# The output product of the last two row groups of an attention kernel, as three one-pass products of exact parts

## The chip, the core and the metric

The kernel runs on one core of one Trainium2 chip. The core has five engines with a queue each: TensorE (PE in the profile, its weight loads PEld), VectorE (DVE), ScalarE (ACT), GpSimd (POOL) and SyncE (SP), which issues most transfers. Each engine works through its own instructions in order and waits on semaphores for the others. Products land in PSUM, eight banks of 128 x 512 float32; everything else lies in SBUF or in device memory. The metric is device microseconds (us) of one execution; lower is better.

## What is computed

Two attention layers over 2048 rows with 576 columns, 32 heads of 18, side by side in the output. Layer A has one key and value head for all 32 query heads and no mask; layer B works in four segments of 512 rows with a memory carried from one to the next.

```python
def _A_ref(x, wq, wk, wv, wo):
    q = (x @ wq).reshape(B, S, H, Dh).transpose(0, 2, 1, 3)
    k = x @ wk
    v = x @ wv
    scores = jnp.einsum("bhqd,bkd->bhqk", q, k) * (Dh ** -0.5)
    p = _softmax(scores, axis=-1)
    o = jnp.einsum("bhqk,bkd->bhqd", p, v)
    return o.transpose(0, 2, 1, 3).reshape(B, S, H * Dh) @ wo
...
return jnp.concatenate([a, b], axis=-1)
```

The change concerns the last line of layer A, the product of the weighed heads with `wo` (576 x 576), for the last two of its four groups of 512 rows.

## The kernel before

A first phase projects both inputs. It splits every float32 operand into a rounded part (`hi`, type float32r) and the exact rest (`lo`), and sums three products, hi x hi, lo x hi, hi x lo, each of which passes through TensorE once (`proj` at line 249, and `values` at line 491, where each product has 128 weight columns taken from the input and 288 or 306 columns of the weights as the moving side). A branch that the drawn inputs do not take follows, and then the attention loop.

The attention loop interleaves scores (L925, L934), exponentials (L943 on ScalarE, some on VectorE) and products with the values (L973). Behind it runs a list of steps that fall due by round: `at` puts a step on the list, `due` emits those whose round `k` has come. For every group of 512 rows, `finish` puts on it: a load of the softmax sums (`sums`, L713, tile `sm`), their reciprocal on VectorE and its store (`inverses`, L726, L731), loads of the raw heads (`load_heads`, L738, tile `o`, two buffers), loads of the inverses (`load_inverses`, L745, tile `rb`) and the multiplication of the heads by them on GpSimd (`weigh`, L758). The 576 head columns are held as five pieces t = 0 to 4, four of 126 rows and one of 72. The last piece holds the last four heads, whose sums come last.

When a group is weighed, its output product `out_proj` joins the list `fill`. It multiplies in plain float32, with 32 weight columns at a time on four column strips of TensorE (`out_part`, L770), 192 output columns per bank and twelve banks per group, each summed over the five pieces; a copy on VectorE takes a bank to the tile `osb` (L795, two buffers) and every third copy is followed by a store (`out_store`, L781). One group is 60 steps (`FILL`). In the attention loop one step runs per round.

What is left at the end of the loop (the rest of the last B group, and the third A group) runs in the ending, eight steps per round, and the last A group follows through all eight banks: six halves of the three tiles `E`, one `O` and one `F`, 288 output columns each, first the pieces 0 to 3 of every bank, then piece 4, then eight copies on ScalarE and VectorE in turn and four stores from tiles of the name `P`.

In this part the order of TensorE, ScalarE and VectorE is the order in which the code emits the instructions (`manual_schedule`, L1093). SyncE's queue is in order too; a tile that is allotted again waits until its last use is over, a store among them.

Of the kernel before, what the change touches and what calls it, by code (L numbers as in the profile page):

```python
# [7 lines left out]
F32 = mybir.dt.float32  # L8
F32R = mybir.dt.float32r
# [3 lines left out]
ALU = mybir.AluOpType  # L13
# [5 lines left out]
S, D, H, DH = 2048, 576, 32, 18  # L19
NSEG, L = 4, 512  # L20
C = 512
# [3 lines left out]
RT = [18 * h for h in HT]  # L25
# [5 lines left out]
PBUFS = 9  # L31
# [40 lines left out]
def attention_pair_kernel(ctx, tc, a_xT, a_w, a_wo, b_xT, b_w, b_wo, b_beta, ident_d, hmask_d, bmask_d, cmask_d, sel_d, zmask_d, selx_d, sely_d, out):  # L72
    nc = tc.nc
# [79 lines left out]
    with ExitStack() as ph:  # L153
# [106 lines left out]
        for c in range(NCH):  # L260
            ready = {}
            if c == 0:
# [11 lines left out]
                for k in range(5):  # L274
# [3 lines left out]
                    for i, (w, x) in enumerate(parts_):  # L278
                        for t in TILES:
# [5 lines left out]
                                start=k == 0 and i == 0,  # L285
# [9 lines left out]
            for t in TILES:  # L295
# [8 lines left out]
                R = RT[t]  # L304
# [54 lines left out]
        for t in range(5):  # L359
            R = RT[t]  # L360
# [405 lines left out]
    def out_part(ab, c, i, t, dst, c0, n, start, stop):  # L766

        for j in range(4):
            r0 = 128 * i + 32 * j
            nc.tensor.matmul(  # L770
                dst[32 * j : 32 * j + 32],
                parts[ab, c][: RT[t], t, r0 : r0 + 32],
                wo[ab][: RT[t], t, c0 : c0 + n],
                start=start,
                stop=stop,
            )

    def out_store(ab, c, i, osb):
        r0 = c * C + 128 * i
        col = 0 if ab == "A" else D  # L780
        nc.sync.dma_start(out[r0 : r0 + 128, col : col + D], osb)  # L781

    def out_proj(ab, c):

        for i in range(4):
            osb = pa.tile([128, D], F32, name="osb", bufs=2)
            for q in range(3):
                cs = slice(192 * q, 192 * q + 192)

                pf = psO.tile([128, C], F32, name="O" if ending and (3 * i + q) % 2 else "F")  # L790
                for t in range(5):
                    out_part(ab, c, i, t, pf[:, :192], cs.start, 192, t == 0, t == 4)
                    if t < 4:
                        yield False
                nc.vector.tensor_copy(osb[:, cs], pf[:, :192])  # L795
                if q == 2:
                    out_store(ab, c, i, osb)
                yield True
# [50 lines left out]
                at(now[0] + 2, 0, lambda: True, store)  # L849
                yield True  # L850

    fill, filled, ending = [], [0], []

    def run_fill(n, whole=False):

        done = 0
        while done < n and fill:
            try:
                full = next(fill[0])
            except StopIteration:  # L860
                fill.pop(0)
                continue
            done += 1
            filled[0] += 1
            if full and not whole:
                break
        return done


    blocksA = [("A", c, hg) for c in range(NCH) for hg in range(8)]  # L870
# [145 lines left out]
    def at(k, cost, ready, step):  # L1016
        later.append((k, cost, ready, step))
        later.sort(key=lambda e: e[0])

    def due(k, most=2, heavy=2):  # L1020

        cost = 0

        near = [its[n][0] for t in turns[k : k + 3] for n, pr in t]
        heavy *= "B" not in near
        for e in [e for e in later if e[0] <= k]:
            if most and cost + e[1] <= heavy and e[2]():
                later.remove(e)
                e[3](k)
                cost += e[1]  # L1030
                most -= 1
        return cost

    def finish(k, ab, c, hg):

        ts = range(4) if hg == 6 else range(4, 5)
        lo, hi = (0, 28) if hg == 6 else (28, 32)
        box, need = {}, 3 if ab == "B" and c > 0 else 1
        weighed.setdefault((ab, c), 0)
        last = (ab, c) == blocks[-1][:2]  # L1040

        d0, d1, d2, d3 = (0, 2, 0, 3) if last else (2, 5, 3, 5) if (ab, c) == ("B", 0) else (2, 5, 3, 6)

        def begin(k):
            assert ab == "A" or c not in LATE_ASK or asked[0] >= c
            summing.add(hg)
            box[0] = sums(ab, c, lo, hi)
            at(k + d1, 0, lambda: True, inv)

        def inv(k):  # L1050
            inverses(ab, c, lo, hi, box[0])
            summing.remove(hg)
            for t in ts:
                at(k, 0, place, lambda k, t=t: load(k, t))

        def place():

            return (ab, c) in parts or len(parts) - filled[0] // FILL < 2 and asked[0] >= min(2, len(parts) + 1)

        def load(k, t):  # L1060
            load_heads(ab, c, t)
            at(k + d2, 0, room, lambda k: weights(k, t))

        def room():

            return loaded[0] + need <= 10

        def weights(k, t):
            loaded[0] += need
            tiles = load_inverses(ab, c, t)  # L1070
            box[t, t] = weigh(ab, c, t, tiles)
            at(k + d3, 1, lambda: True, lambda k: heads(k, t))

        def heads(k, t):
            box[t, t].pop(0)()
            if box[t, t]:
                at(k, 1, lambda: True, lambda k: heads(k, t))
                return
            loaded[0] -= need
            weighed[ab, c] += 1  # L1080
            if weighed[ab, c] == 5 and not last:
                at(k + 2, 0, lambda: True, lambda k: fill.append(out_proj(ab, c)))

        at(k + d0, 0, lambda: hg not in summing, begin)

# [7 lines left out]
    with tc.manual_schedule(engines={ENG.PE, ENG.Activation, ENG.DVE}):  # L1093

        for n, b in enumerate(blocks):
            ms = [m for m in range(len(its)) if block_of[m] == n]
            items = [(m, k) for m in ms for k in range(2)]
            for out_, cut in ((turns, len(items) // 3), (prods, len(items) // 3 - 2)):  # L1100
                at_ = split(len(items), cut)
                out_ += [items[a:z] for a, z in zip(at_, at_[1:])]
        at(ASK + 4, 0, lambda: True, lambda k: load_qf(2))
        for k in range(len(turns) + 2):
            now[0] = k
            exps = [scores(its[n], pr, i == 1) for i, (n, pr) in enumerate(turns[k])] if k < len(turns) else []
            for i in (0, 2, 1) if len(exps) == 3 else range(len(exps)):
                exps[i]()
            if memory is None:
                run_fill(1)  # L1110
            elif k >= ASK and all(its[n][0] == "A" for n, pr in turns[k]) and next(memory, None) is None:
                memory = None

            ends = k > 1 and any(hf and its[n][3] == (NKT - 1 if its[n][0] == "A" else 2) for n, hf in prods[k - 2])
            if slow and (slow[0][0] <= k or not ends):
                slow.pop(0)[2]()
            for n, hf in prods[k - 2] if k > 1 else []:
                ab, c = its[n][:2]
                hg = products(its[n][:3], its[n][3], hf)
                if hg in (6, 7):  # L1120
                    finish(k, ab, c, hg)
                if hg == 7 and ab == "B" and c + 1 < NSEG:
                    load_vseg(c + 1)
            due(k)
            for n, pr in turns[k] if k < len(turns) else []:
                it = its[n]
                ab = it[0]
                if pr == 0:
                    prefetch(ab, keys[ab].index((ab, it[1], it[2] // 2)) + 2)
                    if it in (("A", 0, 2, 8), ("A", 0, 5, 8)):  # L1130
                        load_wo(*(("B", b_wo) if it[2] == 2 else ("A", a_wo)))

        ab, c = blocks[-1][:2]
        ending.append(True)
        while fill:
            due(k, 4)
            run_fill(8, whole=True)
            k += 1
        while weighed[ab, c] < 4:
            due(k, 4)  # L1140
            k += 1
        banks = [psE.tile([128, 2, 512], F32, name="E") for _ in range(3)]
        dst = [bk[:, hf, :288] for bk in banks for hf in range(2)]
        for nm in ("O", "F"):
            bk = psO.tile([128, C], F32, name=nm)
            dst.append(bk[:, :288])
        for g in range(8):
            for t in range(4):
                out_part(ab, c, g // 2, t, dst[g], 288 * (g % 2), 288, t == 0, False)
        while later:  # L1150
            due(k, 4)
            k += 1
        for g in range(8):
            out_part(ab, c, g // 2, 4, dst[g], 288 * (g % 2), 288, False, True)
        for i in range(4):
            osb = pp.tile([128, 2, 512], F32, name="P", bufs=PBUFS)
            for hf in range(2):
                (nc.vector.tensor_copy if hf else nc.scalar.copy)(osb[:, hf, :288], dst[2 * i + hf])
            out_store(ab, c, i, osb[:, :, :288])


# [54 lines left out]
```

## Time and profile before

| | us |
|---|---|
| median of 3 runs | 1428.38 (1427.50 to 1430.46) |
| profiled execution, its time | 1427.14 |
| profiled execution, its span | 1425.4 |
| TensorE busy in the span | 1410.3 |
| ScalarE busy | 1195.2 |
| VectorE busy | 1022.9 |
| GpSimd busy | 247.0 |

The span is what the trace covers; the time also holds what lies around it. Rows of the order of time have the start in us from the span's start, the length in us, the engine, the line of the kernel, the operation, output<-inputs, the shapes, how many instructions were merged, and in brackets the idle time of the engine just before with what ended it. Rows of groups end with busy time in us and mean ns of one, and then the idle time before them. In the trace a float32 product shows as two records, a float32r product as one. The end of a product is modelled; the distance of two starts is what one costs in a stream. SPq rows are the issue of a transfer, not its length.

### The profile page before, as it was taken

The page shows a single profiled execution, that of the slowest core. Times are in us where ns is not written, and L with a number is a line of the kernel's source. Part 1 is how long each engine was busy: PE and PEld are TensorE (multiplying, and loading weights), DVE is VectorE, ACT ScalarE, POOL GpSimd, SP SyncE. Part 2 cuts the span into 40 slices and gives each one's busy share as a digit, 9 for nine tenths or more (in the row PEclk, how much of TensorE's full clock was granted, in tenths as well). Part 3 has the DMA queues.
Part 4 walks back from the last instruction along what each step waited for, and adds up shares of the span by engine and source line. Part 5 has one row for each costly group of instructions (what it writes and reads, how often), then busy time and mean ns, then how long its engine had stood idle before and what let it go on. Part 6 is the DMA issues. An engine that isn't in the chain of part 4 may idle for free.

```text
span 1425.4 us, 41103 instructions
## 1 busy us (share of the span) xinstructions
PE 1410.3 (99%) x17692; PEld 839.5 (59%) x17692; DVE 1022.9 (72%) x1213; ACT 1195.2 (84%) x1429; POOL 247.0 (17%) x326
## 2 busy tenths in 40 slices
PE   9999999999999999999999999999999999999998
PEld 6788888755555555555555555555555555555565
DVE  6556456467787778777777888777778877877761
ACT  4543434489999999999999999999999999999960
POOL 2431000003313214131111150131013300200001
PEclk9999999999999999999999999999999999999999
DMA  9866546457564535232322532231105121110022
GB/s 275 261 215 188 168 143 226 161 165 230 158 202 159 170 109 175 87 108 77 102 68 66 175 118 86 85 114 64 36 34 151 48 78 51 51 43 18 18 87 77
DMA packets 90469, 172.71 MB, mean 121 GB/s; under 512 B 14576, under 2 KB 22377, under 8 KB 89854
## 3 DMA queue, kind: packets, MB, share of 16 engines
q1 hardware_dynamic: 83722, 159.75, 35.8%
q0 software_dynamic: 1664, 4.78, 1.3%
q10 hardware_dynamic: 4896, 5.51, 1.2%
q8 instruction: 140, 2.29, 0.7%
q14 instruction: 47, 0.39, 0.1%
HBM read 99.32 MB, written 70.67 MB: 119 GB/s over the span
## 4 chain that ended last, share of the span: by engine, by line
PE 66%; ACT 9%; issue 2%; DVE 1%; DMA 0%; POOL 0%; DVEq 0%; ACTq 0%
PE O L973 30%; PE E L925 19%; PE F L770 11%; ACT P L943 9%; PE E L934 3%; PE E L770 1%; PE F L827 1%; PE O L770 1%; DVE W L940 1%; DMA out<-osb 0%; DVE osb L795 0%; DVE q L905 0%; DVE q L902 0%; POOL P L948 0%; DVE o L832 0%
## 5 line engine op out<-in xcount | busy, mean ns | idle before, releaser
L943 ACT ACTIVATE P<-E 128x1024 f32<-128x1024 f32 (+1 forms) x800 | 783.3, 1065 | 12.1 <-PE E L925 12.0
L940 DVE COPY W<-E 128x1024 f32<-128x1024 f32 (+1 forms) x384 | 461.2, 1201 | 177.9 <-PE E L925 120.6
L973 PE MATMUL O<-P,VA 128*32 128x256 f32 x7936 | 508.5, 380 | 0.0
L943 ACT ACTIVATE P<-W 128x1024 f32<-128x1024 f32 (+1 forms) x384 | 429.1, 1117 | 2.4 <-DVE W L940 2.2
L973 PEld LDWEIGHTS O<-P,VA 128*32 128x32 f32 x7936 | 262.7, 110 | 146.5 <-issue 5.7
L925 PE MATMUL E<-stA,kstA 56*128 56x512 f32 x1920 | 328.4, 439 | 1.1 <-ACT P L943 0.4
L925 PEld LDWEIGHTS E<-stA,kstA 56*128 56x128 f32 x1920 | 154.9, 184 | 176.3 <-ACT P L943 110.2
L948 POOL TENSOR_SCALAR_AFFINE_SELECT P<-P 128x256 f32<-128x256 f32 (+1 forms) x192 | 94.6, 493 | 474.4 <-ACT P L943 441.5
L758 POOL TENSOR_TENSOR o<-o,rb 126x512 f32<-126x512 f32 (+1 forms) x55 | 81.2, 1490 | 410.7 <-PE F L770 142.2
L770 PE MATMUL F<-woB,o 126*32 126x192 f32 (+1 forms) x1920 | 127.4, 338 | 0.3 <-DVE osb L795 0.3
L905 DVE SCALAR_TENSOR_TENSOR q<-q,PD 128x1024 f32<-128x1024 f32 x96 | 119.3, 1243 | 0.0
L973 PE MATMUL O<-P,vseg 128*32 128x256 f32 (+2 forms) x1536 | 81.4, 344 | 0.0
L770 PEld LDWEIGHTS F<-woB,o 126*32 126x32 f32 (+1 forms) x1920 | 38.2, 108 | 70.8 <-issue 62.4
L770 PE MATMUL F<-woA,o 126*32 126x192 f32 (+1 forms) x1240 | 77.7, 338 | 0.6 <-DVE osb L795 0.6
L982 DVE COPY oe<-O 128x512 f32<-128x512 f32 x64 | 44.3, 692 | 42.6 <-PE O L973 41.2
L118 ACT CAST qp<-pj 126x512 fp32r<-126x512 f32 (+1 forms) x54 | 30.9, 584 | 49.9 <-DVE kmB L447 32.7
L249 PE MATMUL pj<-xh,wBl 128*126 128x512 f32 x180 | 72.3, 403 | 0.0
L249 PE MATMUL pj<-xh,wBh 128*126 128x512 f32 x180 | 71.8, 400 | 0.0
L119 DVE TENSOR_TENSOR qp<-pj,qp 126x512 fp32r<-126x512 f32 (+1 forms) x54 | 36.6, 686 | 37.3 <-ACT qp L118 37.2
L934 PE MATMUL E<-stB 56*128 56x256 f32 (+3 forms) x512 | 61.7, 348 | 1.6 <-ACT P L943 1.1
L973 PEld LDWEIGHTS O<-P,vseg 128*32 128x32 f32 x1536 | 48.8, 109 | 24.3 <-issue 1.6
L934 PEld LDWEIGHTS E<-stB 56*128 56x128 f32 x512 | 38.6, 185 | 32.0 <-ACT P L943 22.3
(182 smaller groups left out, 1366.3 us busy)
## 6 DMA issues: line engine op xcount, KB each, us to landing
stB<-kB SPq DMA_DIRECT2D x96, 144.0 KB
stB<-qB SPq DMA_DIRECT2D x32, 288.0 KB
stA<-qA SPq DMA_DIRECT2D x30, 288.0 KB
oA<-oe SPq DMA_DIRECT2D x32, 256.0 KB
oB<-oe SPq DMA_DIRECT2D x32, 256.0 KB
qA<-qp SPq DMA_DIRECT2D x16, 504.0 KB
kB<-qp SPq DMA_DIRECT2D x16, 504.0 KB
qB<-qp SPq DMA_DIRECT2D x16, 504.0 KB
```

Source lines behind the costliest of these rows:

```text
L119: hold(nc.vector.tensor_tensor(qp[:R, 1, :n], src, qp[:R, 0, :n].bitcast(F32), op=ALU.subtract))
L249: nc.tensor.matmul(dst, w[:, c0 : c0 + M], x, start=i == 0, stop=i == len(ops) - 1)
L758: return lambda: tc.keep_in_program_order(nc.gpsimd.tensor_tensor(dst, a, b, op=op))
L770: nc.tensor.matmul(dst[32 * j : 32 * j + 32], parts[ab, c][: RT[t], t, r0 : r0 + 32], wo[ab][: RT[t], t, c0 : c0 + n], start=start, stop=stop,
L905: steps.append(lambda a=a: v.scalar_tensor_tensor(q, q, a, p, op0=ALU.add, op1=ALU.mult))
L925: nc.tensor.matmul(e[:, j], kstA[rows, 128 * kt : 128 * kt + 128], st[rows, h, :], start=True, stop=True)
L934: nc.tensor.matmul(e[:, j, c0 : c0 + 512 - 128 * k], st[rows, 4 + h, ks], st[rows, h, 128 * k :], start=True, stop=True)
L940: nc.vector.tensor_copy(src[:, :, :n], e[:, :, :n])
L943: nc.scalar.activation(p[:, :, :n], src[:, :, :n], AF.Exp, scale=SCALE)
L948: nc.gpsimd.affine_select(diag, diag, pattern=[[0, 2], [0, m], [1, 128]], base=0, channel_multiplier=-1, compare_op=ALU.is_ge, fill=0.0)
L973: nc.tensor.matmul(o[32 * j : 32 * j + 32, q0 : q0 + n], v, p[:, j % 2, p0 : p0 + n], start=m == hf == 0, stop=last and hf == 1,)
L982: nc.vector.tensor_copy(osb, o)
```

## The change

The ending is rewritten. The group that is under way when the loop ends is finished one step per round of the due list. All groups behind it, here the third and the fourth of layer A, go through a common path:

- the weights `wo` of layer A are split into hi and lo parts, piece by piece, in two tiles of the name `stB`;
- each piece of the weighed heads is split likewise into the two halves of a `P` tile: hi by a copy on ScalarE, lo by a subtraction on VectorE;
- for each piece and each of the eight banks three products follow, 128 rows of the group as weights and 288 columns of `wo` moving;
- eight copies on ScalarE and VectorE in turn take the banks to four tiles, named `W` (two buffers, `bufs=2`) for the third group and `P` for the last, and four stores follow;
- then the next group does the same in the same eight banks.

```diff
-                pf = psO.tile([128, C], F32, name="O" if ending and (3 * i + q) % 2 else "F")
+                pf = psO.tile([128, C], F32, name="F")
...
-        ending.append(True)
-        while fill:
+        while fill and fill[0][0] in begun:
             due(k, 4)
-            run_fill(8, whole=True)
+            run_fill()
+            if filled[0] % FILL == 0:
+                fill.pop(0)
             k += 1
...
+        rows = [key for key, steps in fill] + [blocks[-1][:2]]
+        wparts = [pa.tile([128, 8, C], F32R, name="stB", bufs=2) for _ in range(2)]
+        wh, wl = (w.rearrange("p a b -> p (a b)")[:, : 5 * D].rearrange("p (t d) -> p t d", d=D) for w in wparts)
...
+        def halve(hi, lo, src):
+            nc.scalar.copy(hi, src)
+            nc.vector.tensor_tensor(lo, src, hi.bitcast(F32), op=ALU.subtract)
...
+        def halve_heads(key, t):
+            R = RT[t]
+            x = halves_of[key, t] = pp.tile([128, 2, 512], F32R, name="P", bufs=PBUFS)
+            halve(x[:R, 0], x[:R, 1], parts[key][:R, t])
...
+        def multiply(key, t, dst):
+            R = RT[t]
+            x = halves_of[key, t]
+            for g in range(8):
+                i, c0 = g // 2, 288 * (g % 2)
+                for m, (xp, w) in enumerate(((0, wh), (1, wh), (0, wl))):
+                    nc.tensor.matmul(
+                        dst[g],
+                        x[:R, xp, 128 * i : 128 * i + 128],
+                        w[:R, t, c0 : c0 + 288],
+                        start=t == m == 0,
+                        stop=t == 4 and m == 2,
+                    )
...
+        for n, key in enumerate(rows):
+            end = key == rows[-1]
+            banks = [psE.tile([128, 2, 512], F32, name="E") for _ in range(3)]
+            dst = [bk[:, hf, :288] for bk in banks for hf in range(2)]
+            dst += [psO.tile([128, C], F32, name=nm)[:, :288] for nm in ("O", "F")]
+            for t in range(5):
+                R = RT[t]
+                if n == 0:
+                    halve(wh[:R, t], wl[:R, t], wo["A"][:R, t])
+                if end:
+                    while weighed[key] <= t:
+                        due(k, 4)
+                        k += 1
+                else:
+                    due(k, 4)
+                    k += 1
+                halve_heads(key, t)
+                multiply(key, t, dst)
+            for i in range(4):
+                osb = pp.tile([128, 2, 512], F32, name="P" if end else "W", bufs=PBUFS if end else 2)
+                for hf in range(2):
+                    (nc.vector.tensor_copy if hf else nc.scalar.copy)(osb[:, hf, :288], dst[2 * i + hf])
+                out_store(*key, i, osb[:, :, :288])
```

`run_fill` now runs one step of the first entry of `fill` and records in `begun` which group has been started; its calls in the attention loop do what they did.

More of the change, by code (lines that the diff above doesn't have):

```diff
@@ L850, in ask_memory, with run_fill @@
                 yield True
[L852 to L867, printed above, removed]
+    fill, filled, begun = [], [0], set()
+    def run_fill():
+        while fill:
+            key, steps = fill[0]
+            if next(steps, None) is not None:
+                begun.add(key)
+                filled[0] += 1
+                return
+            fill.pop(0)
     blocksA = [("A", c, hg) for c in range(NCH) for hg in range(8)]
@@ L1081, in heads @@
             if weighed[ab, c] == 5 and not last:
-                at(k + 2, 0, lambda: True, lambda k: fill.append(out_proj(ab, c)))
+                at(k + 2, 0, lambda: True, lambda k: fill.append(((ab, c), out_proj(ab, c))))
         at(k + d0, 0, lambda: hg not in summing, begin)
@@ L1109, in attention_pair_kernel @@
             if memory is None:
-                run_fill(1)
+                run_fill()
             elif k >= ASK and all(its[n][0] == "A" for n, pr in turns[k]) and next(memory, None) is None:
@@ L1131, in attention_pair_kernel @@
                         load_wo(*(("B", b_wo) if it[2] == 2 else ("A", a_wo)))
-        ab, c = blocks[-1][:2]
-        ending.append(True)
-        while fill:
+        while fill and fill[0][0] in begun:
             due(k, 4)
-            run_fill(8, whole=True)
+            run_fill()
+            if filled[0] % FILL == 0:
+                fill.pop(0)
             k += 1
[L1139 to L1159, printed above, removed]
+        rows = [key for key, steps in fill] + [blocks[-1][:2]]
+        assert all(ab == "A" for ab, c in rows)
+        wparts = [pa.tile([128, 8, C], F32R, name="stB", bufs=2) for _ in range(2)]
+        wh, wl = (w.rearrange("p a b -> p (a b)")[:, : 5 * D].rearrange("p (t d) -> p t d", d=D) for w in wparts)
@@ new lines, in halve @@
+        def halve(hi, lo, src):
+            nc.scalar.copy(hi, src)
+            nc.vector.tensor_tensor(lo, src, hi.bitcast(F32), op=ALU.subtract)
+        halves_of = {}
+        def halve_heads(key, t):
[15 more added lines that the diff above has]
+                    )
@@ L1163 @@
+        assert not later
 def kernel(A_x, A_wq, A_wk, A_wv, A_wo, B_x, B_wq, B_wk, B_wv, B_wo, B_beta):
```

## The prediction

> **What bounds the kernel now.** I read the head of the page first, then the chain of waits, then the last 50 us in order of time, because the edit touches nothing earlier: up to the last products of the attention loop both programs have the same instructions in the same order on every engine.
>
> ```profile
> span 1425.4 us, 41103 instructions
> PE 1410.3 (99%) x17692; PEld 839.5 (59%) x17692; DVE 1022.9 (72%) x1213; ACT 1195.2 (84%) x1429; POOL 247.0 (17%) x326
> PE 66%; ACT 9%; issue 2%; DVE 1%; DMA 0%; POOL 0%; DVEq 0%; ACTq 0%
> ```
>
> TensorE (PE) sets the time. Everything that the change can win or lose therefore lies where TensorE's own stream gets shorter or stops. The stage in question, in order of time (columns: start, length, engine, line, output<-inputs, count, and the idle time before with its releaser):
>
> ```profile
> 1376.09 1.22 ACT L943 ACTIVATE P<-W 128x1024 f32<-128x1024 f32 x1
> ...
> 1379.63 1.16 PE L770 MATMUL F<-woB,o 126*32 126x192 f32 x24
> 1379.88 0.69 DVE L982 COPY oe<-O 128x512 f32<-128x512 f32 x1 [3.58 <-PE O L973]
> 1380.60 0.34 SPq L984 DMA_DIRECT2D oA<-oe  x1
> ...
> 1381.04 0.76 SPq L738 DMA_DIRECT2D o<-oA  x1
> ...
> 1381.36 1.83 PE L770 MATMUL F<-woA,o 126*32 126x192 f32 x40 [0.57 <-DVE osb L795]
> 1381.85 0.45 SPq L781 DMA_DIRECT2D out<-osb  x1
> 1382.35 0.76 SPq L738 DMA_DIRECT2D o<-oA  x1
> ...
> 1383.21 0.56 SPq L713 DMA_DIRECT2D sm<-oA  x1
> ...
> 1388.60 1.28 POOL L758 TENSOR_TENSOR o<-o,rb 126x512 f32<-126x512 f32 x1 [0.81 <-DMA o<-oA]
> 1388.75 0.25 DVE L726 RECIPROCAL sm<-sm 128x16 f32<-128x16 f32 x1 [0.25 <-DMA sm<-oA]
> ...
> 1390.33 1.28 POOL L758 TENSOR_TENSOR o<-o,rb 126x512 f32<-126x512 f32 x1 [0.45 <-DMA o<-oA]
> ...
> 1398.60 1.26 POOL L758 TENSOR_TENSOR o<-o,rb 72x512 f32<-72x512 f32 x1 [5.55 <-DMA rb<-rA]
> ...
> 1401.41 11.82 PE L770 MATMUL E<-woA,o 126*32 126x288 f32 x192
> ...
> 1420.33 0.67 PE L770 MATMUL F<-woA,o 72*32 72x288 f32 x8
> 1420.52 0.46 DVE L1158 COPY P<-E 128x288 f32<-128x288 f32 x1 [0.46 <-ACT P L1158]
> 1420.58 0.40 ACT L1158 COPY P<-O 128x288 f32<-128x288 f32 x1
> 1421.06 0.46 DVE L1158 COPY P<-F 128x288 f32<-128x288 f32 x1
> ```
>
> The last B group ends on TensorE at 1380.8. The third A group ("A2") runs from 1381.36 to 1401.41, 20.1 us, the fourth ("A3") to 1421.0, 19.6 us; 4.4 us of copy and store end the span. Note the reciprocal at 1388.75: VectorE waited there for the load of the last softmax sums, 8 us after their source was stored. Before, TensorE had 20 us of A2 to do meanwhile, fed by copies that stand ahead of that reciprocal in VectorE's order.
>
> **What the products become worth.** Each group loses its full-precision products on 32 columns and gets 5 x 8 x 3 = 120 one-pass products of 128 weight columns by 288. The first phase has exactly that kind (two weight parts, two input parts, new weights for every product), and their starts give the price:
>
> ```profile
> 159.09 0.30 PE L491 MATMUL pj<-wBh,xl 128*128 128x288 f32 x1
> ...
> 165.09 0.29 PE L491 MATMUL pj<-wBl,xh 128*128 128x288 f32 x1
> ...
> L491 PEld LDWEIGHTS pj<-wBl,xh 128*128 128x128 f32 x160 | 30.1, 188 | 0.2 <-issue 0.2
> ```
>
> Between the first two rows lie 45 starts, so 6.00 / 45 = 0.133 us each, whatever the 0.3 us of one by itself. A group is 120 x 0.133 = 16.0 us, a piece t (24 products) 3.2 us. Gain on TensorE: 20.1 + 19.6 - 32.0 = 7.7 us. That is all that the change can win.
>
> [...] The rows above show a load of 0.188 us for every product and starts 0.133 us apart, so the loads are hidden there.
>
> **What stands ahead of the first product: the first stall.** Each product needs rounded parts: ScalarE rounds (hi), VectorE subtracts (lo). ScalarE is free at 1376.09 + 1.22 = 1377.3 and its two roundings for t = 0 (0.68 and 0.62) are done by 1378.7, hidden under the last B products. The subtractions are not hidden. In the written order of the engines the tail now runs one output step per round of the due list, not eight, so the reciprocal of the last sums is emitted ahead of the last B copy and of every subtraction. Queued behind that one wait on VectorE are the B copy, ten subtractions, and through them TensorE's second product.
>
> When do the sums land? SyncE's queue changes: the store of 288 KB that stood between the first two loads of A3's heads moves behind the reciprocal, and three head loads of 252 KB now stand ahead of the load of the sums, where there were two and that store. An earlier instance with an empty queue and the landing before bound it:
>
> ```profile
> 1355.73 0.85 SPq L713 DMA_DIRECT2D sm<-oA  x1
> ...
> 1358.27 0.94 DVE L726 RECIPROCAL sm<-sm 112x128 f32<-112x128 f32 x1
> ```
>
> Issue stays near 1383.3 (three issues of 0.76 after 1381.04). Lower bound 1383.3 + 2.5 = 1385.9; upper, behind the third head load and the fourth's share, 1391. Before, the sums landed just behind the second head load (1388.60); with a third load in place of a store of about the same size I take between that and the third's landing (1390.33): 1389.5.
>
> Behind it VectorE does reciprocal 0.25, B copy 0.36, and the first two subtractions, by the nearest rows:
>
> ```profile
> L211 DVE TENSOR_TENSOR xl<-wBl,xh 128x512 fp32r<-128x512 f32 x7 | 4.7, 689 | 5.7 <-ACT xh L205 5.6
> L223 DVE TENSOR_TENSOR wAl<-wBl,wAh 128x618 fp32r<-128x618 f32 x5 | 3.9, 803 | 0.0
> L239 ACT CAST wBh<-wr 128x576 fp32r<-128x576 f32 x5 | 3.4, 680 | 0.0
> L205 ACT CAST xh<-wBl 128x512 fp32r<-128x512 f32 x5 | 3.1, 620 | 4.7 <-DMA wBl<-a_xT 4.7
> ```
>
> 0.75 for 576 columns (between the two rows) and 0.69 for 512: 2.05 us, and 0.15 to reach TensorE (osb ended at 1381.22, its reader began at 1381.36). TensorE resumes at 1389.5 + 2.05 + 0.15 = 1391.7. It has stood since 1380.9 but for one product: 10.8 us. Pieces t = 1 to 4 cost VectorE 1.44 us against 3.2 on TensorE, so they are hidden.
>
> **The clock.** What a stop does to TensorE is shown by the end and the start of the span (columns of the first: window, us, busy of PE, PEld, DVE, ACT, POOL, granted clock, DMA share, GB/s):
>
> ```profile
> 1421.00:1422.00 1.00, 0.00 (x0) 0.00 (x0) 0.46 (x1) 0.00 (x0) 0.00 (x0) 1.00 0.90 316
> 1422.00:1423.00 1.00, 0.00 (x0) 0.00 (x0) 0.00 (x0) 0.00 (x0) 0.00 (x0) 0.84 1.06 372
> 1423.00:1424.00 1.00, 0.00 (x0) 0.00 (x0) 0.00 (x0) 0.00 (x0) 0.00 (x0) 0.50 0.56 198
> ...
> 1.54 4.02 PE L168 MATMUL nd<-sht 128*128 128x512 bf16 x9 [1.54 <-DVE gt L469]
> ...
> 6.51 1.19 PE L281 MATMUL pj<-xh,wAh 128*114 128x512 f32 x4 [0.95 <-ACT wAh L222]
> ```
>
> The clock is halved 1.7 us after the last product (0.84 is 0.68 us at 1.00 and the rest at 0.50). At the start nine products take 4.02 us, 0.45 each, where four of the same width take 1.19 later. So after a stop about 4 us run at half speed: a loss of 2.0 us, bounds 0 and, if it lasts 7 us, 3.5.
>
> [...]
>
> A2 then ends on TensorE at 1391.7 + 15.9 (119 products) + 2.0 = 1409.6.
>
> **The second stall.** A3 uses the same eight banks, and A2's eviction stands ahead of A3's rounding on ScalarE and VectorE. The output tiles are now "W", of which there are two for four stores, so the third pair of copies waits until the first store has been read out; the change adds that wait. The first pair of banks is complete 18 products before the end, 1407.2, and about 0.3 us later visible. In the old ending a pair took 0.98 us from its ScalarE copy to the store's issue:
>
> ```profile
> 1418.21 0.40 ACT L1158 COPY P<-E 128x288 f32<-128x288 f32 x1 [40.90 <-PE E L770]
> 1418.71 0.46 DVE L1158 COPY P<-E 128x288 f32<-128x288 f32 x1 [16.69 <-ACT P L1158]
> ...
> 1419.19 2.77 SPq L781 DMA_DIRECT2D out<-P  x4
> ...
> 1394.87 7.51 SPq L781 DMA_DIRECT2D out<-osb  x3
> ...
> 1399.34 0.36 DVE L795 COPY osb<-O 128x192 f32<-128x192 f32 x1 [2.62 <-DMA out<-osb]
> ```
>
> So the first store goes out at 1408.5, the second 0.8 later at 1409.3. From issue to reuse, a store took 1399.34 - 1394.87 = 4.5 us with another load ahead of it; the last four stores, issued by 1421.6, ended with the span, under 3.8. I take 3.7. The second tile is free at 1413.0; ScalarE copies (0.40) and rounds A3's first piece (0.62), VectorE copies and subtracts (0.69), 1.85 us with the hand-overs: TensorE resumes at 1414.8, 5.2 us after A2. Without the wait for the tiles it would be 1.5. At 5.2 us the clock falls again: 2.0.
>
> A3's own pieces were weighed early, its last one, 11.1 us after the reciprocal (1398.60 + 1.26 against 1388.75), at 1400.6; needed near 1428, so hidden.
>
> **The sum.** 1414.8 + 15.9 + 2.0 = 1432.7; 0.2 to the modelled end and 4.4 of copy and store as before: 1437.3, against 1425.4: +11.9 us. In terms: -7.7 for products, +10.3 for the first stall (1391.7 against 1381.36), +5.2 for the second, +4.0 for the clock, rest roundings. The profiled execution took 1427.14 us, 1.7 more than its span; 1427.14 + 11.9 = 1439.0. The median of the runs shown, 1428.38, is 1.2 higher, so I add half of that: 1439.5.
>
> **The rivals.**
> 1. *The clock stays full across the second stop*, 5.2 us being not long enough, or both losses are small. For it: the record at the start shows 1.00 even though the cadence is half, so the column is not a sure guide. Against: the fall within 1.7 us. One loss less: 1437.5, 18%; both gone: 1435.5, 7%.
> 2. *VectorE isn't held* (the other side): if the subtractions came ahead of the reciprocal's wait, TensorE would resume near 1382.8, with no cold clock there: 8.9 + 2.0 less, 1439.5 - 10.9 = 1428.6, no change. It decides at a start of the A2 products before about 1385. For it speaks only that the sums of an idle queue came in 2.5 us; even so the start would be 1388.1. Chance 5%, with 2% for a result faster than before, where the tiles' wait goes too (1423).
> 3. *The transfers are later*: sums behind all five head loads (1391.8), stores at 4.5 us, half speed for 7 us: +2.3 +0.8 +1.5 to 3: 1445. For it: the head loads in these rows land 1.7 us apart, and the queue is full. Chance 12%.
> 4. *Weight loads show*: if the load's 0.188 us were added to every product, 240 x 0.188 = 45 us more: 1485. The 45 starts speak against it: 1%. [...]
>
> **How the numbers follow.** The forecast with both stalls and both clock losses has 57%, centre 1439.5. The bounds of the landing (-3.6, +1.5), of the stores (-0.4, +0.8) and of the clock (-4, +3) don't all fall together; with rival 1 inside, 1434.5 to 1444.0 leaves out rivals 2 and 4 and most of 3, under 2 in 10. 0.2%, what a measurement can tell from no change here, is 2.9 us: faster 2%, same 4%, slower 94%.
>
> **What would show it.** In the profile after: a gap on TensorE of about 10 us ahead of the first products of stB and P, ended by VectorE, behind a reciprocal that a DMA ended; starts 0.133 us apart once warm and 0.25 just after the gaps; granted clock near 0.5 there; a second gap of 4 to 6 us, with ScalarE's third copy into W ended by the DMA that stores W. Wrong would be: the first of these products running through before 1385, no wait of that copy, or starts 0.2 us apart and more throughout.

## The result and the profile after

| | us |
|---|---|
| before, median of 4 runs | 1429.10 (1427.50 to 1430.46) |
| after, median of 4 runs | 1441.18 (1438.04 to 1441.63) |
| ratio | 1.008, 95% interval 1.0062 to 1.0099 |
| profiled execution after: time, span | 1441.63, 1439.9 |

The change makes the kernel 12 us slower, 0.8%, and the interval leaves out 1. The forecast was 1439.5, with 1434.5 to 1444.0.

The head of the page after the change (busy time, share of the span, instructions), with the row of the granted clock in 40 slices:

```profile
span 1439.9 us, 40019 instructions
PE 1407.7 (98%) x17132; PEld 847.2 (59%) x17132; DVE 1036.6 (72%) x1220; ACT 1204.8 (84%) x1448; POOL 248.8 (17%) x326
PEclk9999999999999999999999999999999999999989
```

TensorE is busy for 2.6 us less than before and the span is 14.5 us longer, so it stands still for longer than before. The last 60 us in order of time, columns as before:

```profile
1383.59 1.16 PE L770 MATMUL F<-woB,o 126*32 126x192 f32 x24
...
1384.56 0.34 SPq L978 DMA_DIRECT2D oA<-oe  x1
1384.68 0.40 PE L1156 MATMUL E<-stB,P 126*128 126x288 f32 x1
1385.00 2.56 SPq L738 DMA_DIRECT2D o<-oA  x3
1387.66 0.56 SPq L713 DMA_DIRECT2D sm<-oA  x1
1392.74 0.25 DVE L726 RECIPROCAL sm<-sm 128x16 f32<-128x16 f32 x1 [8.21 <-DMA sm<-oA]
1393.04 2.99 POOL L758 TENSOR_TENSOR o<-o,rb 126x512 f32<-126x512 f32 x2 [0.39 <-DMA o<-oA]
1393.12 1.80 DVE L1141 TENSOR_TENSOR stB<-woA,stB 126x576 fp32r<-126x576 f32 x1
1394.84 1.75 DVE L1141 TENSOR_TENSOR P<-o,P 126x512 fp32r<-126x512 f32 x1
1396.51 0.75 DVE L1141 TENSOR_TENSOR stB<-woA,stB 126x576 fp32r<-126x576 f32 x1
1396.64 4.19 PE L1156 MATMUL E<-stB,P 126*128 126x288 f32 x17 [11.56 <-DVE P L1141]
1397.18 0.68 DVE L1141 TENSOR_TENSOR P<-o,P 126x512 fp32r<-126x512 f32 x1
1401.47 2.55 PE L1156 MATMUL E<-stB,P 126*128 126x288 f32 x18
...
1404.66 2.56 PE L1156 MATMUL E<-stB,P 126*128 126x288 f32 x18
...
1413.04 4.12 SPq L781 DMA_DIRECT2D out<-W  x4
...
1415.35 0.40 ACT L1185 COPY W<-E 128x288 f32<-128x288 f32 x1 [2.04 <-DMA out<-W]
...
1417.89 3.85 PE L1156 MATMUL E<-stB,P 126*128 126x288 f32 x17 [0.33 <-DVE P L1141]
...
1422.38 2.56 PE L1156 MATMUL E<-stB,P 126*128 126x288 f32 x18
```

The first product, which needs hi parts alone, runs at 1384.68. The next waits 11.56 us for VectorE, whose own wait of 8.21 us is for the load of the last sums, at the reciprocal. Behind it the first two subtractions take 1.80 and 1.75 us while GpSimd multiplies, the next two 0.75 and 0.68. The starts of two pieces, 1401.47 and 1404.66, are 3.2 us apart. The piece just after the stop takes 4.8 (1396.64 to 1401.47, less one product). At 1415.35 ScalarE's third copy has waited 2.04 us for the store out of `W`, and A3's stream begins at 1417.89. Its first piece takes 4.5 us. The granted clock in windows (window, us, busy of PE, PEld, DVE, ACT, POOL, clock, DMA share, GB/s):

```profile
1388.00:1390.00 2.00, 0.00 (x0) 0.00 (x0) 0.00 (x0) 0.00 (x0) 0.00 (x0) 1.00 0.45 175
1390.00:1391.00 1.00, 0.00 (x0) 0.00 (x0) 0.00 (x0) 0.00 (x0) 1.00 (x1) 0.57 0.46 164
...
1396.00:1398.00 2.00, 1.36 (x5) 1.36 (x6) 2.00 (x4) 0.00 (x0) 0.04 (x1) 0.50 0.08 28
...
1417.00:1418.00 1.00, 0.51 (x2) 0.30 (x2) 0.86 (x2) 1.00 (x3) 0.00 (x0) 0.72 0.85 298
1418.00:1419.00 1.00, 1.00 (x4) 1.00 (x5) 1.00 (x3) 1.00 (x3) 0.00 (x0) 0.50 0.90 308
```

The clock is halved at 1390.1, 5 us after TensorE stopped, and again at about 1417.4, 3 us after the second stop began. Both streams start at half speed.

Below, "the ending" is the time from the start of the last B products (here 1383.59) to the end of the span; it leaves out what varies ahead of it. It grew from 45.8 us (1425.4 - 1379.63) to 56.3, by 10.5.

### The profile page after: what moved, and what is told of

Read it like the earlier page. It is cut to its first block, busy times and chain, and to the rows that moved or that the text cites. A ratio compares the mean times of both kernels' runs of the same rounds, so it can differ in the third digit from the quotient of the medians.

```text
span 1439.9 us, 40019 instructions
## 1 busy us (share of the span) xinstructions
PE 1407.7 (98%) x17132; PEld 847.2 (59%) x17132; DVE 1036.6 (72%) x1220; ACT 1204.8 (84%) x1448; POOL 248.8 (17%) x326
## 4 chain that ended last, share of the span: by engine, by line
PE 66%; ACT 8%; issue 2%; DMA 2%; DVE 1%; SPq 0%; DVEq 0%; ACTq 0%
PE O L967 30%; PE E L919 19%; PE F L770 10%; ACT P L937 8%; PE E L928 3%; PE E L1156 2%; PE F L826 1%; DMA sm<-oA 1%; DMA stB<-qB 0%; DVE W L934 0%; DMA oA<-oe 0%; PE F L1156 0%; PE O L1156 0%; DMA stB<-kB 0%; SPq L738 0%
## 5 line engine op out<-in xcount | busy, mean ns | idle before, releaser
L770 PE MATMUL F<-woA,o 126*32 126x192 f32 (+1 forms) x960 | 63.9, 338 | 0.0
```

The costliest lines, as they stand in the source:

```text
L770: nc.tensor.matmul(dst[32 * j : 32 * j + 32], parts[ab, c][: RT[t], t, r0 : r0 + 32], wo[ab][: RT[t], t, c0 : c0 + n], start=start, stop=stop,
```

## The experiments

| kernel | ending, us | first stop ends, us into the ending | ratio to before, interval |
|---|---|---|---|
| before, three traces | 45.8, 45.6, 45.5 | | 1 |
| changed, two traces | 56.3, 56.7 | 13.1, 13.4 | 1.0080 (1.0062 to 1.0099), 1.0076 (1.0064 to 1.0088) |
| e1: split first | 43.8 | 2.3 | 0.9991 (0.9981 to 1.0001) |
| e2: more tiles | 53.4 | 13.4 | 1.0054 (1.0034 to 1.0074) |
| e3: keep busy | 54.7 | 13.2 | 1.0076 (1.0056 to 1.0096) |
| e4: sums first | 51.3 | 7.0 | 1.0040 (1.0025 to 1.0055) |
| e5: e1 and e2 | 40.5 | 2.3 | 0.9965 (0.9952 to 0.9978) |
| e6: e5, and A3 split ahead | 39.0 | 2.3 | 0.9960 (0.9947 to 0.9973) |

Each edit is against the changed kernel.

**e1: split first.**

```diff
-        while fill and fill[0][0] in begun:
-            due(k, 4)
-            run_fill()
...
+        halve_first(0)
+        rounds = 0
+        while fill and fill[0][0] in begun:
+            run_fill()
...
+            rounds += 1
+        for t in range(1, 5):
+            halve_first(t)
+        for _ in range(rounds):
+            due(k, 4)
+            k += 1
```

`halve_first(t)` splits the piece t of `wo` and of the third group.

> Theory (VectorE is held at the reciprocal of the last sums, and the subtractions of the parts are queued behind it): with the third group's parts split ahead of the due steps that emit the reciprocal, TensorE stops for 1 to 2 us instead of 11.6 between the last B product and the products of stB and P, and its clock there stays full, so the first 24 products take 3.2 us and not 4.8; the second stop of 3.6 us stays. About 10 + 1.7 us less than the changed kernel: 1428 to 1431. Rival (TensorE waits for ScalarE's roundings, for the banks or for the heads, not for VectorE's queue): the gap stays above 8 us and the time at 1438 to 1442.

In order of time:

```profile
1380.08 0.69 DVE L976 COPY oe<-O 128x512 f32<-128x512 f32 x1 [3.58 <-PE O L967]
...
1380.68 0.75 DVE L1134 TENSOR_TENSOR stB<-woA,stB 126x576 fp32r<-126x576 f32 x1
...
1381.35 0.68 DVE L1134 TENSOR_TENSOR P<-o,P 126x512 fp32r<-126x512 f32 x1
...
1382.09 2.53 PE L1166 MATMUL E<-stB,P 126*128 126x288 f32 x17 [0.77 <-DVE P L1134]
...
1388.79 0.25 DVE L726 RECIPROCAL sm<-sm 128x16 f32<-128x16 f32 x1 [1.41 <-DMA sm<-oA]
```

The same reciprocal still waits for the same load until 1388.79, but nothing that TensorE needs is queued behind it. The stop is 0.77 us, and the piece after it takes 3.2 us. The ending is 12.7 us shorter than the mean of the two traces of the change, 1426.23 us against 1426.72 for the kernel before on that chip: no difference that can be measured. VectorE's order was the cause of the first stop; the rival falls.

**e2: more tiles.**

```diff
-                osb = pp.tile([128, 2, 512], F32, name="P" if end else "W", bufs=PBUFS if end else 2)
+                osb = pp.tile([128, 2, 512], F32, name="P", bufs=PBUFS)
```

> Theory (the second stop is the wait of the third copy for one of two W tiles, which is free only when its store has been read out): with the third group's four output tiles taken from the nine P tiles the third copy runs at once, and the second stop falls from 3.6 us to about 1.6 (last copy, rounding, subtraction). If the clock then stays full, the last group's first 24 products take 3.2 us and not 4.5. 2.0 us less for the wait and 0 to 1.3 for the clock: 1437.5 to 1439.5. The first stop stays at 11 to 12 us. Rival (the stop is the rounding and subtraction of the last group's parts behind the copies, whatever the tiles): stop above 3 us, time unchanged at 1440 to 1442.

```profile
1411.63 0.56 PE L1156 MATMUL F<-stB,P 72*128 72x288 f32 x3
...
1412.86 0.40 PE L1156 MATMUL E<-stB,P 126*128 126x288 f32 x1 [0.66 <-ACT P L1140]
...
1413.58 2.53 PE L1156 MATMUL E<-stB,P 126*128 126x288 f32 x17 [0.33 <-DVE P L1141]
...
1416.75 2.56 PE L1156 MATMUL E<-stB,P 126*128 126x288 f32 x18
```

No copy waits for a store. From the end of A2's last product (1411.63 + 0.40) to the resumed stream it is 1.6 us instead of 3.6, and the next piece takes 3.2 us (1413.58 to 1416.75), so the clock held. The ending is 3.1 us shorter, 1435.75 us in time. That is below the expected range, but the kernel before took 1426.72 us beside it, not 1429.10: the distance of 9.0 us lies within the expected one of 8.4 to 10.4.

**e3: keep busy.**

```diff
+                if n == t == 0:
+                    for d in range(78):
+                        nc.tensor.matmul(
+                            dst[d % 6], halves_of[key, t][:R, 0, 0:128], wh[:R, t, 0:288], start=True, stop=True
+                        )
                 multiply(key, t, dst)
```

> 78 extra one-pass products into six banks that the first real product of each bank overwrites, placed behind the first rounded part, fill some 10.4 us of the first stop; their results are not used. Theory (a stop halves TensorE's clock, and the products behind it pay for that): the products behind the stop begin at the same place, about 12 us behind the last B product, but the first 24 take 3.2 us instead of 4.8: 1.6 us less than the changed kernel, about 1439.5, and the granted clock stays at 1.00 through the first stop. Rival (the slow first products are the wait for the second part of each operand, not the clock): the first 24 still take over 4 us, and the time is 1441.

```profile
1380.88 10.54 PE L1183 MATMUL E<-stB,P 126*128 126x288 f32 x78
...
1393.02 2.52 PE L1156 MATMUL E<-stB,P 126*128 126x288 f32 x17 [1.48 <-DVE P L1141]
...
1396.18 2.56 PE L1156 MATMUL E<-stB,P 126*128 126x288 f32 x18
```

```profile
1380.00:1391.00 11.00, 11.00 (x101) 10.60 (x94) 2.15 (x4) 2.85 (x6) 3.88 (x4) 1.00 0.37 128
1391.00:1395.00 4.00, 2.52 (x20) 2.29 (x19) 4.00 (x6) 0.00 (x0) 1.42 (x1) 1.00 0.30 108
```

(The second fence is the view by windows.) The products resume as late as in the change, 13.2 us into the ending, the clock stays at 1.00, and the first piece takes 3.2 us instead of 4.8. The ending is 1.8 us shorter than the changed kernel's mean of 56.5; in the times, with their intervals, this does not show. The slow first piece is the clock.

**e4: sums first.** The load of the last sums is put ahead of the loads of A3's heads:

```diff
-        nc.sync.dma_start(sm[:R, 0], o_d[c][lo:hi, 0, :].rearrange("h (s t) -> h s t", t=w))
+        lastsum[0] = nc.sync.dma_start(sm[:R, 0], o_d[c][lo:hi, 0, :].rearrange("h (s t) -> h s t", t=w))
...
+        with tc.issue_after(lastsum[0].ins) if (ab, c) == ("A", NCH - 1) else nullcontext():
...
+            if last and hg == 6 and 7 not in begun_sums:
+                return False
```

> The load of the last softmax sums is issued ahead of the loads of the last group's heads. Theory (the length of the first stop is set by the landing of that load, which three head loads of 252 KB stand ahead of): the reciprocal comes 3 to 4 us sooner after the last B product, and the two subtractions behind it, which took 1.80 and 1.75 us beside GpSimd's multiplications, take 0.75 and 0.69 as these multiplications move later: first stop 6 to 7 us instead of 11.6, about 1436. Rival (the load of the sums waits for its source's store, not for the queue): the reciprocal moves by less than 1 us, the time stays at 1439 to 1442.

```profile
1382.53 0.34 SPq L980 DMA_DIRECT2D oA<-oe  x1
...
1384.70 0.58 SPq L714 DMA_DIRECT2D sm<-oA  x1
...
1386.77 0.25 DVE L727 RECIPROCAL sm<-sm 128x16 f32<-128x16 f32 x1 [4.27 <-DMA sm<-oA]
...
1387.15 0.74 DVE L1149 TENSOR_TENSOR stB<-woA,stB 126x576 fp32r<-126x576 f32 x1
...
1387.81 0.68 DVE L1149 TENSOR_TENSOR P<-o,P 126x512 fp32r<-126x512 f32 x1
...
1388.55 4.45 PE L1164 MATMUL E<-stB,P 126*128 126x288 f32 x17 [5.50 <-DVE P L1149]
...
1390.08 1.49 POOL L760 TENSOR_TENSOR o<-o,rb 126x512 f32<-126x512 f32 x1 [144.69 <-DMA o<-oA]
...
1394.24 2.60 PE L1164 MATMUL E<-stB,P 126*128 126x288 f32 x18
```

The sums are 2.1 us from issue to use (1384.70 to 1386.77) where they were 5.1 (1387.66 to 1392.74), and the two subtractions, now ahead of GpSimd's work, take 0.74 and 0.68. The stream resumes 7.0 us into the ending instead of 13.1, but the ending is only 5.2 us shorter than the changed kernel's mean, because the first piece behind the stop is slower: 5.7 us (1388.55 to 1394.24) instead of 4.8; its 23 products start 0.25 us apart, those of the next piece 0.135 (1394.24 to 1397.48). What is left of the wait has the rival's mechanism: the load goes out 2.2 us after its source's store was issued (1382.53), and SyncE stands for 1.8 of them (1382.87 to 1384.70), with that store under way.

**e5 and e6.** e5 has both edits of e1 and e2. e6 also splits A3's pieces 0 and 1 ahead of A2's copies:

```diff
+            if not end:
+                halve_last(0)
+                halve_last(1)
             for i in range(4):
                 osb = pp.tile([128, 2, 512], F32, name="P", bufs=PBUFS)
```

> Both edits together: the third group's parts split ahead of the reciprocal, and its output tiles taken from the nine P tiles. Theory (the two stops and the clock that they cost are all that hides the 7.7 us of shorter products): no stop over 1.6 us, the clock stays full, both groups' pieces at 3.2 us each; some 3 us less than with the first edit alone, so about 0.2% below the kernel before: ratio 0.996 to 0.9985. Rival (something else in the new ending costs time, such as the stores or the last copies): ratio 0.999 to 1.001, as with the first edit alone.

> As both edits together, and the last group's pieces 0 and 1 are split ahead of the third group's copies, so that TensorE can go on as banks come free. Theory: the second stop falls from about 1.4 us to under 0.5 us, the ending from the last B products to the end of the span is 7 us shorter than before's 45.8 us: ratio 0.994 to 0.997. Rival (the second stop is the banks' eviction, not the order of splits and copies): the stop stays over 1 us and the time equals that of the two edits.

Order of time of e6:

```profile
1394.47 2.56 PE L1166 MATMUL E<-stB,P 72*128 72x288 f32 x18
...
1397.67 2.56 PE L1166 MATMUL E<-stB,P 126*128 126x288 f32 x18
...
1400.87 2.56 PE L1166 MATMUL E<-stB,P 126*128 126x288 f32 x18
```

A2's last piece, A3's first and second start 3.2 us apart: there is no second stop. In e5 it was 1.6 us. The ratio of e5, 0.9965, lies in the range expected for it, and its interval leaves out the 0.999 of its rival. The ending of e6 is 39.0 us, 6.6 less than the mean of before's three (45.6), and e6 is faster than both kernels: 1422.05 us against 1427.38 for the kernel before. The medians of e5 (1422.28) and e6 don't differ by more than their intervals; the endings, of one trace each, differ by 1.5 us, where those of the three traces of the kernel before lie within 0.3.

**The changed kernel again, and the kernel before again.**

> The changed kernel itself, unedited, beside the others on the same chip: theory 1.007 to 1.009 of the kernel before, with a first stop of 11 to 13 us and a second of 3 to 4 us, the length of the first varying with the landing of the last sums.

> The kernel before itself, traced again, because in all traces of the new ending but one the time differs from before's by about 1.5 us more than the ending does. If the ending of before (45.8 us from the start of the last B products to the end of the span) varies, this trace gives another length, 44.5 to 47; if the part ahead of it varies, the last B products begin elsewhere than at 1379.6, between 1379 and 1384.

> The kernel before, traced a third time, for the spread of the same two numbers: ending 45.8 us within 0.5, last B products from 1379 to 1384.

The changed kernel took 1439.53 us, ratio 1.0076. Before's ending was 45.6 and 45.5 us in its two new traces, its last B products began at 1379.55 and 1380.73. In the two traces of the changed kernel they begin at 1383.59 and 1382.47, behind the same instructions in the same order. So of the 12 us in time, 10.5 to 11 are in the ending.

The traces show two places ahead of the ending where the two traces of the changed kernel lose time. The first is the start of the program. The same four products, in the kernel before and in the changed kernel:

```profile
7.77 1.09 PE L281 MATMUL pj<-xl,wAh 128*114 128x512 f32 x4
```

```profile
8.34 1.91 PE L281 MATMUL pj<-xl,wAh 128*114 128x512 f32 x4
```

The view by windows of the changed kernel has the granted clock at 0.50 there:

```profile
8.00:9.00 1.00, 1.00 (x4) 0.79 (x3) 0.92 (x2) 0.37 (x2) 0.00 (x0) 0.50 1.04 388
```

Behind this start the changed kernel is 1.87 us later than the first trace of before, and 1.95 in its second trace. None of the other nine traces has it, although e1 to e6 have the same instructions up to there. The second place is a reciprocal of earlier sums in the attention loop, which waits for their load just as the one in the ending does:

```profile
1362.42 0.95 DVE L726 RECIPROCAL sm<-sm 112x128 f32<-112x128 f32 x1 [1.84 <-DMA sm<-oA]
```

The wait is 1.84 and 1.83 us in the two traces of the changed kernel, 1.36 and 1.62 in two of the kernel before and none in its first, and between none and 1.73 in e1 to e6. SyncE held this load back for the store of its source, for 3.8 us here and 1.9 in the first trace of before. The wait comes and goes in both kernels, so it isn't the change. Whether the runs without a trace have these losses, and why they come, is open.

## Why the prediction was right

Its direction, both stops with their causes and the loss of the clock held. Three sizes were off, in part against each other, and one cause of time was not in it: that GpSimd would slow VectorE down.

- *Products at 0.133 us, a piece at 3.2*: measured 3.2 in every piece behind a full clock. In the profile after, every one of these products has a weight load of its own, of 188 ns at the median (L1156), and 24 products start within the 3.19 us from 1401.47 to 1404.66, 0.133 apart: the loads are hidden. Rival 4 falls. Most of the gain of 7.7 us is there: e6, which still waits 0.77 us for VectorE ahead of its second product, has 6.6 of it.
- *The first stop, held by the reciprocal*: forecast to end 12.1 us after the start of the last B products (1391.7 - 1379.63), measured 13.1. The sums came sooner than assumed (reciprocal 9.2 us into the ending, not 9.9). The mis-sized term is the pair of subtractions: 1.44 us by rows of the first phase, 3.55 measured, because GpSimd's multiplications of A3 ran at the same time. e4 has the same pair without them at 1.42. No rival had this.
- *Rival 2, VectorE isn't held*, was priced at no change (1428.6); e1 makes it so, and it is no change (0.9991). In the changed kernel itself it did not hold.
- *The clock, 2.0 us for each stop*: 1.8 and 1.4 (4.83 and 4.49 us for 23 products that take 3.07 at full clock). e3 shows that the first is the clock. e1's first stop (0.77 us) and e2's second (1.6) cost nothing of the kind; the granted clock was 1.00 through both (1380 to 1386 in e1, 1411 to 1415 in e2). Rival 1 falls for both stops.
- *The second stop, 5.2 us*: 3.6, less than the 4 to 6 named as its sign. The wait for the `W` tile is the one named (e2), but the store freed its tile in 2.3 us (1413.04 to 1415.35), not 3.7. The rows that it was priced from had other transfers beside them, which may be why; nothing tests that. This is the largest error.
- *Rival 3, later transfers*: the sums and the stores were sooner than forecast; its centre of 1445 was not reached.
- *The sum*: +11.9 us forecast for the ending, +10.5 measured: 1.0 more for the first stop, 0.8 less for the clock, 1.6 less for the second stop. In time the change is +12.1 (1441.18 - 1429.10). What the ending lacks was made up by time ahead of it, which the forecast did not contain, so that the time came out within 2 us of it is partly luck.

## What to carry to other kernels

A cheaper product can lose more than it saves if its operands must be made by an engine whose queue is held by something slower: before counting the saving, write down the order of each engine that the new work passes through, and look for a wait on a transfer ahead of it. When the order of emission is changed to please one engine, as the rounds were here, read it again for all others. The stop of 3.6 us on TensorE cost 1.4 more than its length here, and moving the producers (e1, e6) was worth far more than filling the stop (e3).

## What the runs showed of the hardware

- VectorE's subtraction of two SBUF operands and GpSimd's multiplication held each other up where they ran at the same time. Beside GpSimd the subtraction took 1.80 and 1.75 us instead of 0.75 and 0.68; in e1, where VectorE was subtracting in a row, it was GpSimd that lost:

```profile
1386.03 0.74 DVE L1134 TENSOR_TENSOR stB<-woA,stB 72x576 fp32r<-72x576 f32 x1
1386.48 2.05 POOL L758 TENSOR_TENSOR o<-o,rb 126x512 f32<-126x512 f32 x1 [143.05 <-DMA o<-oA]
1386.70 0.68 DVE L1134 TENSOR_TENSOR P<-o,P 72x512 fp32r<-72x512 f32 x1
...
1388.72 1.29 POOL L758 TENSOR_TENSOR o<-o,rb 126x512 f32<-126x512 f32 x1 [0.19 <-DMA o<-oA]
```

  GpSimd's multiplication took 2.05 us there, and 1.29 at 1388.72 with no subtraction beside it. What makes one wait for the other no run here shows.
- The delay from TensorE's stop to the halved clock was not constant: 1.7 us at the end of the kernel before (1421.0 to 1422.7), 5 and 3 us in the two stops of the changed kernel (1385.1 to 1390.1, 1414.3 to 1417.4). What sets it no run here shows.
